# A sum moved behind a step's value products, and the outputs' halves and turn moved behind the probabilities' own

## The chip, the cores and the metric

The kernel runs on one core of a Trainium2 chip. The metric is the device time of one execution in microseconds, and a kernel's time is the median of several runs. The core has a matrix engine (TensorE, PE in the rows), a vector engine (DVE), an activation engine (ACT), a general engine (POOL), and SyncE (SP), which here does nothing but issue transfers. Each engine takes its instructions in the order in which the program gives them.

## The reference

Two stages follow each other. The first is block-sparse attention over 4 batches, 8 heads, 768 positions and a head width of 64, in blocks of 32. A block of queries sees its neighbours, the first and last block, and three sampled blocks; the first and the last block of queries see all. The second is a feed-forward stage over the 3072 x 512 result:

```python
scores = np.where(mask, scale * q @ k.T, -1e9)
attn = softmax(scores)
x = (attn @ v) as 3072 x 512
h = x @ w_in                              # 512 x 2048
g = h * erf(softplus(h))
out = g @ w_out                           # 2048 x 512
```

## The kernel before

The feed-forward products and those with the values work on halves: a float32 matrix is held as a 16-bit high half and a 16-bit low half (what the high half leaves out), and a product is made of three products of halves. Before the values of a batch can be split, they are scaled by a power of two that follows from their sum of squares.

The main loop (line 1022) has a pass for each of 96 groups of the feed-forward stage, and two more to empty it. A group is 256 tokens by 256 of the 2048 columns. Each pass, called a step here, issues for the feed-forward stage: `ff_first` (24 products, `h<-xT,wi`), `ff_logs` (five activations on ACT), `ff_gate` of the group before (DVE, makes `g`), `ff_second` of the group two before (`o<-wo,g`, 12 products) and, after the eighth group of a token block, `ff_store`, which empties the two output banks `o` into `wo`'s spare rows, one on ACT and one on DVE. Many steps also advance the attention stage by one unit (a set of queries of half the heads): `scores` (PE, into the single bank pair `s`), `soft_max` (DVE), `soft_exp` (ACT, `pf`), `soft_low` (DVE: a cast to the high half from the thirteenth unit on, and the subtraction that gives the low half of `p`) and `soft_turn` (a transposing transfer on SP's queue, `pT<-p`). Two units later `values` multiplies `pT` by gathered values `vb` into the bank `po_bank`, `norm` (DVE) scales it into `xf`, and, when both halves of the heads are there, `turn` takes over: ACT copies `xf` to a high half, DVE subtracts for the low half (`x<-xf,x`), and SP's queue turns both (`xT<-x`). `ff_first` of a later token block reads `xT`.

A batch's values are prepared while the batch before is worked on. `behind` (line 853) puts parts into a list, and the next step runs them as `ready`: a first part (`high`) early in the step and a second (`low`) late. `scale_v` (line 239) is a first part: it sums the squares over the partitions with a product by ones, `whole_sum` (line 194), and turns the sum into a scale with four small DVE instructions, `m_v`, `e_v`, `s_v`, `i_v`. `high_v` is another first part: ACT multiplies by that scale. The sum is written to the last column of the bank that `values` uses:

```python
po_bank = ps_po.tile([P, 512], F32, tag="po", name="po_bank")
whole = po_bank[:, 511:]                                    # whole_sum
po = po_bank[:, : 4 * (D + 1)].rearrange(...)               # values
```

Outside the preparation ahead of the loop `scale_v` runs six times, twice for each later batch. In five of these steps there is a `values` as well. `turn` does something in every step whose `values` completes a set of heads, 24 times in all, 22 of them with a turn on SP's queue.

Nothing reorders the program: each engine's list, SP's queue of transfers included, is what the lines give in their order.

Of the kernel before, what the change touches and what calls it, by code (L numbers as in the profile page):

```python
# [43 lines left out]
def sparse_attention_moe(ctx: ExitStack, tc: tile.TileContext, qT, kT, v, sampled, w_in, w_out, out):  # L44
# [125 lines left out]
    def transpose(out, x):  # L170

        if not on_pe[0]:
            sp.dma_start_transpose(out=out, in_=x)
            return
        for k in range(0, x.shape[1] // P, 8):
            t = ps_o.tile([P, 512], F32, tag="o", name="turned").bitcast(F16).rearrange("p (k c) -> p k c", c=P)
            for j in range(8):
                c = (k + j) * P
                pe.transpose(t[:, j], x[:, c : c + P], unity)
            act.activation(out[:, k : k + 8], t, AF.Copy)  # L180
# [73 lines left out]
    def write_values():  # L254
        for write in writes:
            sp.dma_start(*write)
        writes.clear()
# [272 lines left out]
    def work(steps):  # L530

        for step in steps.split():
            kind, key, k = step[0], step[1], step[2:]
            steps_of[kind](key, *([int(k)] if k else []))
# [42 lines left out]
    def soft_turn(unit):  # L577

        p2, _, _, n = softs.pop(unit)
        tag = "_".join(str(x) for x in unit)  # L580
        if unit[0] == "e":
            pT = at.tile([P, 8, P], F16, tag="pe", name=f"pT_{tag}", bufs=1)
        else:
            pT = at.tile([P, 16, P], F16, tag="pT", name=f"pT_{tag}", bufs=3)[:, : 2 * n // P]
        transpose(pT, p2)
        pts[unit] = pT
# [109 lines left out]
    def turn(b, t, quad):  # L696
        if quad == 1:
            xf = xfs.pop((b, t))
            x2 = at.tile([P, 2, DM], F16, tag="x2", name=f"x2_{b}_{t}", bufs=1)
            xr = xf.rearrange("p h d -> p (h d)")  # L700
            act.activation(x2[:, 0], xr, AF.Copy)
            dve.tensor_tensor(x2[:, 1], xr, x2[:, 0], ALU.subtract)
            ch, u = divmod(t, CT)
            if u == 0:
                xTs[b, ch] = mo.tile([P, 2 * NK, CT, P], F16, tag="xT", name=f"xT_{b}_{ch}", bufs=3)
            transpose(xTs[b, ch][:, :, u, :], x2.rearrange("p a s -> p (a s)"))
# [20 lines left out]
    def ff_first(b, ch, fg):  # L727
        tag = f"{b}_{ch}_{fg}"
        isg = first_scale(b)
        h = ps_h.tile([P, W], F32, tag="h", name=f"h_{tag}")  # L730
        xT = xTs[b, ch].rearrange("p n u c -> p n (u c)")
        for j in range(FG):
            f = fg * FG + j
            hj = h[:, j * CW : (j + 1) * CW]
            for kt in range(NK):
                i, c = (f // 4) * NK + kt, (f % 4) * P
                hi, lo = wi16[:, i, c : c + P], wi16[:, i, 512 + c : 512 + c + P]
                xa, xb = xT[:, kt], xT[:, NK + kt]
                pe.matmul(hj, hi, xa, start=kt == 0, stop=False)
                pe.matmul(hj, hi, xb, start=False, stop=False)  # L740
                pe.matmul(hj, lo, xa, start=False, stop=kt == NK - 1)
        ffs[b, ch, fg] = (h, isg)
# [3 lines left out]
    def ff_logs(b, ch, fg):  # L746

        h, isg = ffs[b, ch, fg]
        tag = f"{b}_{ch}_{fg}"
        x = mo.tile([P, W], F32, tag="x", name=f"x_{tag}")  # L750
        act.activation(x, h, AF.Relu, bias=H_CAP, scale=isg)
        act.activation(x, x, AF.Exp, bias=H_CAP, scale=-1.0)
        act.activation(x, x, AF.Ln, bias=1.0, scale=C0)
        q = mo.tile([P, W], F32, tag="s", name=f"q_{tag}", bufs=2)
        act.activation(q, x, AF.Square, bias=C2)
        act.activation(x, x, AF.Ln, bias=1.0, scale=C4)
        ffs[b, ch, fg] = (h, x, q)

    def ff_power(b, ch, fg):
        h, x, q = ffs[b, ch, fg]  # L760
        dve.scalar_tensor_tensor(q, x, C3 / C1, q, ALU.mult, ALU.add)
# [5 lines left out]
    def ff_gate(b, ch, fg):  # L767
        h, _, hs = ffs.pop((b, ch, fg))
        scale = 2.0**-H_SHIFT
        dve.scalar_tensor_tensor(hs, hs, -1.0, h, ALU.add, ALU.mult)  # L770
        g = mo.tile([P, 2, W], F16, tag="g", name=f"g_{b}_{ch}_{fg}", bufs=FF_LAG + 1)
        dve.tensor_scalar(g[:, 0], hs, scale, None, ALU.mult)
        dve.scalar_tensor_tensor(g[:, 1], hs, scale, g[:, 0], ALU.mult, ALU.subtract)
        gs[b, ch, fg] = g
# [34 lines left out]
    def write_results():  # L809
        for result in results:  # L810
            sp.dma_start(*result)
        results.clear()
# [14 lines left out]
    def gathers(m):  # L827

        nonlocal kfree, vfree
        if kjobs and kfree >= 4 and kjobs[0][0] in have_k:  # L830
            kfree -= 4
            gather(*kjobs.pop(0))
        room = 4 if begun > 0 else VGS
        while vjobs and vjobs[0][0] in have_v:
            b, i = vjobs[0]
            n = 2 if i > 0 else 1
            fresh = b > 0 and 0 < i < VGS
            if vfree < n or room < n * (1 + fresh):
                break
            vfree -= n  # L840
            room -= n * (1 + fresh)
            vjobs.pop(0)
            gather_v(b, i) if i > 0 else whole_v(b, -1 - i)

    def next_queries(m):

        b, n = divmod(m, per)
        if n < 9 and n % 2 == 1:
            load_q(b, n // 2 + 2)
        if n == per - 1 and b + 1 < B:  # L850
            load_q(b + 1, 1)
# [38 lines left out]
    def seen(unit):  # L890

        if unit[0] == "m":
            return unit[1:]
        if unit[0] == "f" and unit[2] % 2 == 1:
            return unit[1], MT, unit[2] // 2
        return None

    def used_keys(unit):
        nonlocal kfree
        if unit[0] == "m" and unit[3] == 1:  # L900
            kfree += 4
        elif unit[0] == "e" and unit[2] == 1:
            kfree += 4
# [6 lines left out]
    def unit_of(n):  # L910
        return units[n] if 0 <= n < len(units) else None

    def values_of(place):
        nonlocal vfree
        values(*place)
        if place[2] == 1:
            vfree += 4 if place[1] < MT else 5
# [104 lines left out]
    for m in range(len(groups) + FF_LAG):  # L1022
        ch, i = divmod(m, NGR)
        steps = 0
        if ch < len(until):
            first = until[ch - 1] if ch else FIRST
            steps = first + -(-(until[ch] - first) * (i + 1) // NGR) - begun
        elif begun < len(units) + PV_LAG:
            steps = 1
        assert steps in (0, 1)  # L1030
        group = groups[m] if m < len(groups) else None
        last = groups[m - 1] if 0 < m <= len(groups) else None
        unit = unit_of(begun) if steps else None
        old = unit_of(begun - PV_LAG) if steps else None
        place = seen(old) if old and begun - PV_LAG >= FIRST else None
        begun += steps
        write_values()
        write_results()
        if group:
            ff_first(*group)  # L1040
            ff_logs(*group)
        ready, prepared[:] = prepared[:], []
        for high, _ in ready:
            if high:
                high()
        if place:
            values_of(place)
        if steps:
            gathers(begun)
        if unit:  # L1050
            scores(unit)
            used_keys(unit)
        if last:
            ff_gate(*last)
        if place:
            norm(*place)
        if m < len(EARLY):
            work(EARLY[m])
        if m >= FF_LAG:
            for u in range(CT):  # L1060
                ff_second(*groups[m - FF_LAG], u)
        if unit:
            soft_max(unit)
            next_queries(begun - 1)
        if group:
            ff_power(*group)
        for _, low in ready:
            if low:
                low()
        if unit:  # L1070
            soft_exp(unit)
        if group:
            ff_exp(*group)
        if m < len(AMID):
            work(AMID[m])
        if m >= FF_LAG:
            for u in range(CT):
                ff_store(*groups[m - FF_LAG], u)
        if place:
            turn(*place)  # L1080
        if unit:
            soft_low(unit)
            soft_turn(unit)
        if m < len(LATE):
            work(LATE[m])
        if unit:
            behind(begun - 1)
# [37 lines left out]
```

## Time and profile before

| | us |
|---|---|
| median of 3 runs | 824.81 |
| lowest and highest | 823.09, 825.76 |
| the profiled execution | 830.67 |
| its span, first to last instruction | 828.9 |
| mean granted clock of TensorE | 0.932 |

The profiled execution is one run, taken with the profiler on; its own time stands 0.7% above the median. Rows of the trace are times within its span.

### The profile page before, as it was taken

What the parts mean: (1) busy time and instruction counts of PE and PEld (TensorE: products, weight loads), DVE (VectorE), ACT (ScalarE), POOL (GpSimd) and SP (SyncE); (2) the same over time, 40 slices, a digit from 0 to 9 for tenths busy, and PEclk for the clock granted to TensorE, in tenths of its full rate; (3) what the DMA queues carried; (4) which work ended last, traced back from release to release, by engine and by line L of the source; (5) the groups of instructions that cost most, each with busy time, mean ns of one, the idle gap of its engine ahead of it and who ended that gap; (6) DMA issues with size and microseconds to landing.
All of it is one profiled execution on the core that took longest, in us unless ns stands there. A gap on an engine that the chain in (4) does not pass through costs nothing. (4 is left out here: it accounts for less than half of the span.)

```text
span 828.9 us, 26604 instructions
## 1 busy us (share of the span) xinstructions
PE 698.3 (84%) x10852; PEld 463.3 (56%) x10852; DVE 576.0 (69%) x1019; ACT 552.9 (67%) x943; POOL 126.0 (15%) x343
## 2 busy tenths in 40 slices
PE   1353645889986979899999897999999999999997
PEld 1133423555654656566666665666676665666664
DVE  3993696988755866775677876776677767754454
ACT  4553567997555757676678767667677676676774
POOL 4621030202211221010011121100111110000000
PEclk9975766999998999899999999999999999999999
DMA  8999971797598889782478899762687968220000
GB/s 306 290 278 273 252 176 32 162 213 167 143 173 191 207 194 211 146 184 63 111 181 195 176 193 231 155 123 43 163 188 168 181 115 187 41 52 20 1 26 26
DMA packets 199498, 129.24 MB, mean 156 GB/s; under 512 B 143952, under 2 KB 167120, under 8 KB 199376
## 3 DMA queue, kind: packets, MB, share of 16 engines
q1 hardware_dynamic: 195952, 115.74, 62.4%
q0 software_dynamic: 3424, 11.80, 4.5%
q8 instruction: 85, 1.39, 0.7%
q14 instruction: 37, 0.30, 0.1%
HBM read 81.52 MB, written 12.95 MB: 114 GB/s over the span
## 5 line engine op out<-in xcount | busy, mean ns | idle before, releaser
L60 PE MATMUL h<-xT,wi 128*128 128x256 f16 x2304 | 274.7, 276 | 12.0 <-ACT wi L60 5.3
L60 PE MATMUL o<-wo,g 128*128 128x512 f16 x1152 | 271.5, 386 | 7.4 <-ACT wo L60 4.0
L60 PEld LDWEIGHTS <-wi 128*128 128x128 f16 x2304 | 227.6, 99 | 64.0 <-ACT wi L60 6.5
L60 PEld LDWEIGHTS <-g 128*128 128x128 f16 x1152 | 109.3, 99 | 148.5 <-issue 33.9
L60 ACT ACTIVATE x<-x 128x512 f32<-128x512 f32 x288 | 181.5, 630 | 9.1
L60 POOL COPY keys<-keys 128x128 f32 x264 | 90.0, 391 | 287.7 <-PE s_m L60 246.8
L60 ACT ACTIVATE x<-h,isg 128x512 f32<-128x512 f32 x96 | 65.9, 686 | 95.5 <-PE h L60 95.4
L60 DVE SCALAR_TENSOR_TENSOR q<-x,q 128x512 f32<-128x512 f32 x96 | 68.0, 708 | 66.5 <-ACT x L60 66.3
L60 ACT ACTIVATE pf_m<-s_m,nb_m 128x256 f32<-128x256 f32 x160 | 62.7, 474 | 57.0 <-DVE nb_m L60 54.1
L60 PE MATMUL po_bank<-vb,pT_m 128*32 128x65 f16 (+1 forms) x3840 | 46.4, 205 | 40.7 <-DMA vb<-vtab 16.2
L60 DVE SCALAR_TENSOR_TENSOR q<-q,h 128x512 f32<-128x512 f32 x96 | 65.5, 682 | 20.2 <-ACT q L60 20.2
L60 ACT ACTIVATE q<-q 128x512 f32<-128x512 f32 x96 | 60.6, 632 | 25.6 <-DVE q L60 25.5
L60 PE MATMUL s_m<-keys,qt 64*32 64x192 f32 (+1 forms) x1600 | 70.7, 359 | 6.9 <-ACT pf_m L60 4.1
L60 DVE SCALAR_TENSOR_TENSOR g<-q,g 128x512 f16<-128x512 f32 x96 | 66.5, 692 | 3.3
L60 PEld LDWEIGHTS <-pT_m 128*32 128x32 f16 x3840 | 40.1, 101 | 50.8 <-issue 19.5
L60 DVE TENSOR_REDUCE mx_m<-s_m 128x4 f32<-128x1024 f32 x40 | 48.8, 1220 | 20.4 <-PE s_m L60 19.9
L60 ACT ACTIVATE q<-x 128x512 f32<-128x512 f32 x96 | 60.5, 630 | 3.0
L60 PEld LDWEIGHTS s_m<-keys,qt 64*32 64x32 f32 (+1 forms) x1600 | 45.8, 135 | 18.1 <-ACT pf_m L60 5.0
L60 DVE TENSOR_TENSOR p_m<-pf_m,p_m 128x1024 f16<-128x1024 f32 x40 | 49.0, 1226 | 3.2 <-ACT p_m L60 2.1
L60 DVE TENSOR_SCALAR g<-q 128x512 f16<-128x512 f32 x96 | 41.1, 428 | 3.3
L60 POOL COPY keys<-wi 128x768 f32<-128x768 f32 (+1 forms) x24 | 17.0, 737 | 167.7 <-DMA wi<-in_kT_dram 167.7
L60 DVE TENSOR_TENSOR x<-xf,x 128x512 f16<-128x512 f32 x24 | 16.8, 700 | 33.6 <-ACT x L60 33.6
(113 smaller groups left out, 533.7 us busy)
## 6 DMA issues: line engine op xcount, KB each, us to landing
vb<-vtab SPq DMA_DIRECT2D x280, 65.0 KB, 3.0
vb<-vtab SPq DMA_DIRECT2D x32, 390.0 KB, 4.4
vtab<-vn SPq DMA_DIRECT2D x16, 390.0 KB, 6.8
vb<-vtab SPq DMA_DIRECT2D x12, 520.0 KB, 5.5
vraw<-in_v_dram SPq DMA_DIRECT2D x7, 768.0 KB, 6.0
qt<-in_qT_dram SPq DMA_DIRECT2D x20, 256.0 KB, 4.3
out_dram<-wo SPq DMA_DIRECT2D x20, 256.0 KB, 4.3
vb<-vtab SPq DMA_DIRECT2D x36, 130.0 KB, 3.1
```

What stands on the lines that cost most here:

```text
L60: done = call(*args, **kwargs)
```

## The change

Two calls are moved. `values_of(place)` goes ahead of the loop over the first parts, so that on TensorE the sum for the values' scale comes behind the step's value products (DVE's and ACT's own order stays the same by this). `turn(*place)` goes behind `soft_low(unit)` and `soft_turn(unit)`: on DVE the subtraction for the outputs comes behind the cast and subtraction for the probabilities, and on SP's queue `xT<-x` behind `pT<-p`. ACT has nothing in `soft_low` and `soft_turn`, so its order stays. No instruction is added or left out.

```diff
         ready, prepared[:] = prepared[:], []
+        if place:
+            values_of(place)
         for high, _ in ready:
             if high:
                 high()
-        if place:
-            values_of(place)
         if steps:
             gathers(begun)
...
-        if place:
-            turn(*place)
         if unit:
             soft_low(unit)
             soft_turn(unit)
+        if place:
+            turn(*place)
         if m < len(LATE):
             work(LATE[m])
```

## Rows read from the trace of the kernel before

**Rows 1.** The page's first part: busy time, share, instructions.

```profile
PE 698.3 (84%) x10852; PEld 463.3 (56%) x10852; DVE 576.0 (69%) x1019; ACT 552.9 (67%) x943; POOL 126.0 (15%) x343
```

**Rows 2.** Waits: who waited for whom; total us, times, longest us.

```profile
DVE x L60 <- ACT x L60: 33.6, 24, 2.1
...
PE po_bank L60 <- DMA vb<-vtab: 16.2, 7, 8.1
...
PE po_bank L60 <- DVE m_v L60: 11.2, 6, 4.5
PE po_bank L60 <- DMA pT_m<-p_m: 10.5, 6, 3.4
```

**Rows 3.** Windows: length, busy us by engine, granted clock, DMA share, GB/s.

```profile
680.20:687.90 7.70, 7.69 (x141) 4.85 (x140) 5.65 (x10) 5.06 (x10) 0.00 (x0) 1.00 0.66 195
331.80:345.70 13.90, 10.11 (x143) 6.04 (x142) 10.11 (x23) 8.60 (x16) 0.46 (x1) 0.75 0.87 188
508.00:522.90 14.90, 10.45 (x144) 6.10 (x143) 11.08 (x23) 9.16 (x17) 1.32 (x3) 0.77 0.84 180
470.00:482.10 12.10, 9.20 (x173) 5.93 (x172) 7.61 (x14) 7.52 (x16) 3.46 (x10) 0.86 1.24 225
160.00:180.00 20.00, 17.88 (x398) 11.21 (x399) 18.45 (x29) 18.35 (x28) 1.71 (x7) 0.91 0.91 191
```

**Rows 4.** Timeline around the step at 331.8: start, length, instruction, idle before.

```profile
333.19 1.57 ACT L60 ACTIVATE pf_m<-s_m,nb_m 128x256 f32<-128x256 f32 x4 [0.93 <-DVE nb_m L60]
...
334.43 0.28 PE L60 MATMUL po_bank<-one,top_v 128*128 128x1 f32 x2
...
335.83 0.69 DVE L60 TENSOR_TENSOR x<-xf,x 128x512 f16<-128x512 f32 x1 [2.14 <-ACT x L60]
...
337.16 1.23 DVE L60 TENSOR_TENSOR p_m<-pf_m,p_m 128x1024 f16<-128x1024 f32 x1
...
338.30 0.15 DVE L60 TENSOR_SCALAR m_v<-po_bank 128x1 f32<-128x1 f32 x1
...
338.51 1.50 PE L60 MATMUL po_bank<-vb,pT_m 128*32 128x65 f16 x96 [3.79 <-DVE m_v L60]
...
342.81 0.96 DVE L60 TENSOR_REDUCE mx_f<-s_f 128x1 f32<-128x768 f32 x1 [1.34 <-PE s_f L60]
...
345.96 0.75 DVE L60 TENSOR_SCALAR wo<-o,iso 128x512 f32<-128x512 f32 x1
```

**Rows 5.** Timeline of DVE in the step at 508.0.

```profile
523.38 0.75 DVE L60 TENSOR_SCALAR wo<-o,iso 128x512 f32<-128x512 f32 x1
```

**Rows 6.** Timeline at waits for turned probabilities: SP's queue and PE.

```profile
292.90 1.24 SPq L60 DMA_TRANSPOSE xT<-x  x1
294.22 2.29 SPq L60 DMA_TRANSPOSE pT_m<-p_m  x1
...
298.80 1.22 PE L60 MATMUL po_bank<-vb,pT_m 128*32 128x65 f16 x96 [3.36 <-DMA pT_m<-p_m]
...
649.71 0.96 PE L60 MATMUL po_bank<-vb,pT_m 128*32 128x65 f16 x96 [1.22 <-DVE g L60]
...
692.48 1.09 PE L60 MATMUL po_bank<-vb,pT_m 128*32 128x65 f16 x96 [1.74 <-DMA pT_m<-p_m]
693.50 0.83 PE L60 MATMUL s_e<-keys,qt 64*64 64x64 f32 x24
```

**Rows 7.** Timeline of SP's queue and PE ahead of the second token block.

```profile
173.31 4.09 SPq L60 DMA_TRANSPOSE pT_m<-p_m  x1
...
183.57 0.71 PE L60 MATMUL h<-xT,wi 128*128 128x256 f16 x5
```

**Rows 8.** Time from issue to landing: all pT, one xT, one pT.

```profile
DMA to landing us min/median/max: 4.3/5.2/10.1
...
xT<-x SPq DMA_TRANSPOSE x1, 5.5
...
pT_m<-p_m SPq DMA_TRANSPOSE x1, 5.6
```

## The prediction

> **What bounds the kernel now.** I read the page first: TensorE (PE) is busy for 84% of the span, more than any other engine [rows 1]. A mean hides the stages, so next come the waits of each engine, then windows of one step each. A step is one pass of the main loop; it begins with its 24 products `h<-xT,wi`, and I name it by the time at which these begin. The quiet step at 680.2 (24 `h`, 96 products of `values`, 8 of a full row's scores, 12 `o`) takes 7.7 us with PE busy for 7.69 of them at full clock [rows 3]: PE sets the pace, and a step gets shorter only where PE stands still or runs slowly.
>
> PE's waits inside the loop nearly all stand before `po_bank`, that is, before the first product of `values`. They have three causes: DVE's `m_v` (11.2 us in 6 waits), the turned probabilities `pT` (10.5 us) and the gathered values `vb` (16.2 us) [rows 2]. The change touches the first two. The waits' own length is not all they cost. The step at 331.8 takes 13.9 us and that at 508.0 takes 14.9, with mean granted clocks of 0.75 and 0.77, between the two levels of 1.2 and 2.4 GHz [rows 3]: PE stands for 3.79 us [rows 4] and 4.5 us, the longest of the six [rows 2], and what follows runs slowly: the 96 products take 1.50 us [rows 4].
>
> **Part one: the sum behind `values`.** Now the order on PE is `h`, `whole_sum` (two passes, 0.28 us), `values`. The sum's column is in `po_bank`, the tile that `values` writes, so `values` waits until DVE's `m_v` has read the sum. At 338.51 the first product starts 0.06 us after `m_v` ends [rows 4]. `m_v` is late because DVE does it in order, behind the previous step's tail: it waits 2.14 us for ACT's copy of the outputs, then does x's low half (0.69) and, until 337.16 + 1.23 = 338.39, the cast and the subtraction of `p_m`, 2.56 us in all, 1.9 of them for `p_m` [rows 4].
>
> With the sum behind `values`, PE has no reader to wait for: `values` can run at 334.4, the sum at 335.4, the scores at 335.8. The scores need the exponentials that began at 333.19 to be done, four in 1.57 us, so by 334.8 [rows 4]. The step costs the quiet 7.7 plus 0.3 for the sum, 8.0. That gives 13.9 - 8.0 = 5.9 us here and 14.9 - 8.0 = 6.9 us at 508.0, which has the same form [rows 3]. Together 12.8 us, clock included.
>
> What is late next: the following step's first `o` needs the output banks, emptied by the two `wo<-o` of this step. DVE's ends at 345.96 + 0.75 = 346.7, and at 524.1 in the other step [rows 4, 5]. In the new order DVE's tail is 0.9 us shorter (part two) and the 1.34 us that DVE's `mx_f` waited for PE's scores are gone [rows 4], so these end near 344.5 and 521.9. PE gets there at 331.8 + 8.0 and 4.4 more, 344.2: 2.6 for the 24 `h` (331.8 to 334.43), 0.96 for `values` and 0.83 for an edge row's scores [rows 4, 6]. In the other step it is 520.4. New waits of 0.3 and 1.5 us: 12.8 - 1.8 = 11.0 us.
>
> The other three steps of this kind in the loop have `m_v` waits under a microsecond (the 11.2 us less 3.79 and 4.5 leave 2.9 for four, one of them ahead of the loop, where the order stays). I count nothing for them: two lie just ahead of the `pT` waits at 298.8 and 475.7, which would take back what they give, and in the third DVE is short of time. Bounds: 0 and 1.6 us. The cost of this part lies on DVE: `m_v`, and behind it the gate, `norm`, the maximum and the scale for ACT's halves, wait for `values` to end, about 1 us later where DVE was early. The gate's product is read by PE a step later, so this is hidden in a quiet step; where it is not, it costs up to 1 us, once.
>
> **Part two: `turn` behind `soft_low` and `soft_turn`.** Nothing is added or removed. On DVE the low half of `p` no longer waits behind x's: the exponentials are done at 334.8, the cast and the subtraction (1.9) end at 336.7, x's low half follows at 336.7 to 337.4, and `m_v` comes at 337.4 instead of 338.30. DVE's waits before `x` (33.6 us in 24 [rows 2]) are filled with that work. ACT's order stays the same. On SP's queue the turn of `p` is issued ahead of the turn of x.
>
> At four places PE waits for a `pT` whose issue stood right behind an `xT`: 3.36, 1.22 (put down to DVE's g there, but `pT`, issued at 644.1, lands 5.6 us later [rows 8], at that moment) and 1.74 us [rows 6], and the 2.9 us that PE is not busy in the step at 470.0 [rows 3]. The `xT` ahead holds the queue for 294.22 - 292.90 = 1.32 us [rows 6]; at the other three the same two rows are 1.32, 2.72 and 1.68 us apart. Earlier by that much, and no more than the wait itself: 1.32 + 1.32 + 1.22 + 1.68 = 5.5 us. The rest of the 10.5 us lies mostly before 180, but there DVE is busy for 18.45 of 20 us [rows 3] and gives back only its own wait before x; with the later `m_v` against it I count 1.0 us, bounds 0 and 2.2.
>
> The clock may add to this. The step at 470.0 keeps PE busy for 9.20 us where a quiet one needs 7.69 [rows 3], so slow clock costs 1.5 us after a 2.9 us stall, while after 1.22 us the products run at full speed (0.96 us for 96 [rows 6]). For the stalls of 1.6 and 2.0 us that would be left no row tells; bounds 0 and 3.0 us for both, and I take 0, since the stalls are cut and not gone. On this the Trainium skill, "TensorE: Matmul & The Clock Gate", section "What's actually happening", says that the monitor's window runs freely, not from the start of the kernel, so that equal stalls need not cost the same: by it the sum could be 1.5 or 3.0 us better.
>
> What it costs: x's turn lands later, by the turn of `p` ahead of it. The feed-forward first reads it two or more steps later nearly everywhere. The tightest is the step at 183.57: there `pT` takes the queue for 4.09 us from 173.31 [rows 7], right behind x's turn, which is issued at 172.0 and lands 5.5 us later [rows 8]; later by 4.1 it lands at 181.6, still 2 us ahead. That margin covers the early gain, not more.
>
> **Sum.** 11.0 + 5.5 + 1.0 = 17.5 us. From this I take 1.0 for the `pT` of the steps after 331.8 and 508.0: PE now comes there 5.9 us sooner, `pT` only 1.5 us. Issued near 336.8, it lands at the median of 5.2 us [rows 8] at 342.0, when PE wants it at 342.4, and the other step is alike; by the extremes (4.3 and 10.1 us) each step loses 0 or up to 5. Net 16.5 us. The profiled execution took 830.67 us (span 828.9, 1.8 around it) and would take 814.2; the median of the runs is 0.7% below it, and 824.81 - 16.5 = 808.3. I forecast 808.
>
> **The rivals.** (a) `pT` takes the place of `m_v`: in the two steps after the long stalls it lands as late as the slow ones, and each gives back about 3 us: 808 + 6 = 814. For it: the spread of the landings [rows 8]; against: 0.4 us of room at the median. Chance 0.13.
> (b) The order of issue doesn't reach the landing, since both turns run at once: the four gains of 5.5 fall away, and (a) loses its 1.5 us of help: about 815. The Trainium skill, "DMA: Bandwidth & Descriptors", section "Two DMAs through the same engine are not ordered", says that nothing orders transfers across the 16 engines; by that rule this is the case to expect. Against it, the queue's own rows: a turn's issue takes 1.24 to 4.09 us and the next begins only behind it [rows 6, 7]. Chance 0.12.
> (c) Slower: `m_v` is now behind everything that `values` waits for. Where gathers are late in such a step, the stall holds DVE's whole queue and ACT's scale too. Five steps carry a sum and `values`; above 3.3 us in each the 16.5 us are gone. The `vb` waits have a mean of 2.3 us and reach 8.1 [rows 2]; at 5.2, between the two, the kernel takes 808 + 26 = 834. For it: gathers wait on the same queue; against: in none of the five steps is a gather the last wait now. Chance 0.06.
> (d) No change: PE's place is taken by another equal wait (the output banks or the scores' bank), 824.8. The scores' bank is free in time by the rows, the output banks are in the sum. Chance 0.07.
>
> **How the numbers follow.** The forecast has 0.62. Runs of this kernel differ by 0.3%, so 0.3% is what can be told: faster means under 822.3. Forecast, (a) and (b) are faster, 0.87; (d) same, 0.07; (c) slower, 0.06. The low end adds the clock's 3.0, the small steps' 1.6, the early 1.2 and the 1.0 taken off: 801. The high end takes (a) and (b) with 5 us more for both together: 820. Cases (c) and (d) stay outside.
>
> **What the new profile would show.** Right: `DVE m_v` gone from PE's waits in the loop; the steps that held 13.9 and 14.9 us at 8 to 9.5 with the clock at 1.00; DVE's waits before `x` under 10 us; `pT` waits smaller by half. Wrong: an equal wait for `pT` or `vb` before `po_bank`, PE waiting for `wo` before `o` by more than 2 us, or PE waiting for `xT` before `h`.

## The result and the profile after

The changed kernel takes 815.0 us (median of 6 runs, 810.17 to 818.35), the kernel before 825.2 beside it (6 runs). The ratio is 0.9861 with an interval of 0.9829 to 0.9892: 11.5 us less, between 8.9 and 14.1 (differences in time are here and below the ratio's share of the median of before; the two medians differ by 10.2). The forecast was 808 in a range of 801 to 820, from a gain of 16.5 us. The side and the range were right, the gain was put too high.

The profiled execution took 814.35 us, its span is 812.6 us with a mean granted clock of 0.954 (before: 828.9 and 0.932). First the page's line of busy time, then the waits of both engines (total us, times, longest us).

```profile
PE 689.7 (85%) x10852; PEld 458.3 (56%) x10852; DVE 575.1 (71%) x1019; ACT 551.1 (68%) x943; POOL 126.5 (16%) x343
```

```profile
PE po_bank L60 <- DMA vb<-vtab: 15.5, 8, 6.6
...
PE po_bank L60 <- DMA pT_m<-p_m: 3.6, 4, 2.3
...
DVE x L60 <- ACT x L60: 3.1, 4, 1.2
...
PE s_f L60 <- ACT pf_m L60: 2.6, 2, 1.5
...
PE po_bank L60 <- DVE m_v L60: 1.3, 1, 1.3
```

Against [rows 2]: DVE's waits before `x` fell from 33.6 to 3.1 us, those of PE for `m_v` from 11.2 in 6 to one of 1.3 ahead of the loop, those for `pT` from 10.5 to 3.6. The gathers kept theirs (16.2, 15.5). One line is new: PE waits, in two steps, before a full row's scores `s_f` until ACT has done the exponentials `pf_m`. PE's busy time fell by 8.6 us [rows 1] with the same 10,852 instructions, so part of the gain is clock.

The timeline of the step that began at 331.8 before (start, length, instruction, idle before) and windows of it, of the one at 508.0 and of the one at 470.0, whose beginnings are now 326.4, 495.4 and 461.6:

```profile
317.84 1.01 SPq L60 DMA_DIRECT2D vraw<-in_v_dram  x1
...
323.32 0.84 ACT L60 ACTIVATE vj<-vraw 128x768 bf16<-128x768 f32 x1 [3.59 <-DMA vraw<-in_v_dram]
...
325.25 0.15 DVE L60 TENSOR_REDUCE top_v<-vsq 128x1 f32<-128x2 f32 x1 [4.80 <-ACT vj L60]
...
328.39 1.22 DVE L60 TENSOR_REDUCE mx_m<-s_m 128x4 f32<-128x1024 f32 x1
...
329.10 0.96 PE L60 MATMUL po_bank<-vb,pT_m 128*32 128x65 f16 x96
...
329.90 1.57 ACT L60 ACTIVATE pf_m<-s_m,nb_m 128x256 f32<-128x256 f32 x4 [0.94 <-DVE nb_m L60]
...
329.99 0.38 PE L60 MATMUL po_bank<-one,top_v 128*128 128x1 f32 x2
...
331.52 1.51 PE L60 MATMUL s_f<-keys,qt 64*64 64x512 f32 x8 [1.15 <-ACT pf_m L60]
...
332.23 1.23 DVE L60 TENSOR_TENSOR p_m<-pf_m,p_m 128x1024 f16<-128x1024 f32 x1
...
333.48 3.56 SPq L60 DMA_TRANSPOSE pT_m<-p_m  x1
...
333.97 0.15 DVE L60 TENSOR_SCALAR m_v<-po_bank 128x1 f32<-128x1 f32 x1
...
337.14 1.25 SPq L60 DMA_TRANSPOSE xT<-x  x1
...
338.83 0.96 PE L60 MATMUL po_bank<-vb,pT_m 128*32 128x65 f16 x96 [0.49 <-DVE q L60]
...
340.80 1.46 PE L60 MATMUL o<-wo,g 128*128 128x512 f16 x6 [0.25 <-ACT wo L60]
```

```profile
326.40:335.60 9.20, 8.05 (x144) 5.08 (x143) 7.79 (x18) 8.04 (x15) 1.89 (x5) 1.00 0.65 186
495.40:504.95 9.55, 8.06 (x143) 5.05 (x142) 8.14 (x18) 8.24 (x16) 1.81 (x5) 1.00 0.64 183
461.60:469.85 8.25, 7.69 (x174) 5.30 (x173) 6.74 (x13) 5.89 (x12) 1.87 (x5) 1.00 1.35 233
```

Both parts change the order as they say. `values` starts at 329.10 without a wait, 4.9 us ahead of `m_v` (in [rows 4] it began 0.06 us behind it), and `pT` is issued ahead of `xT`. The 13.9, 14.9 and 12.1 us of [rows 3] are 9.2, 9.55 and 8.25, at a clock of 1.00. What stands in the way now is read upward from 331.52: the scores wait for the exponentials (331.47), these for `mx_m` on DVE, and DVE had stood for 4.80 us before `top_v`, with `mx_m` queued behind it, because ACT's squares `vj` waited 3.59 us for the raw values `vraw`, issued at 317.84. The prediction did not look at these squares; in the step at 331.8 of before they come at 326.62 (ACT, timeline of before):

```profile
326.62 0.84 ACT L60 ACTIVATE vj<-vraw 128x768 bf16<-128x768 f32 x1 [1.47 <-DMA vraw<-in_v_dram]
```

### The profile page after: what moved, and what is told of

It reads as the page before. It is cut to its first block, busy times and chain, and to the rows that moved or that the text cites. A ratio compares the mean times of both kernels' runs of the same rounds, so it can differ in the third digit from the quotient of the medians.

```text
span 812.6 us, 26628 instructions
## 1 busy us (share of the span) xinstructions
PE 689.7 (85%) x10852; PEld 458.3 (56%) x10852; DVE 575.1 (71%) x1019; ACT 551.1 (68%) x943; POOL 126.5 (16%) x343
## 5 line engine op out<-in xcount | busy, mean ns | idle before, releaser
L60 PE MATMUL h<-xT,wi 128*128 128x256 f16 x2304 | 273.7, 276 | 13.9 <-ACT wi L60 7.4
L60 POOL COPY keys<-keys 128x128 f32 x264 | 92.0, 396 | 286.2 <-PE s_m L60 249.1
L60 PE MATMUL s_m<-keys,qt 64*32 64x192 f32 (+1 forms) x1600 | 67.5, 347 | 6.3 <-ACT pf_m L60 4.1
L60 PE MATMUL po_bank<-vb,pT_m 128*32 128x65 f16 (+1 forms) x3840 | 44.3, 202 | 22.1 <-DMA vb<-vtab 15.5
L60 DVE TENSOR_REDUCE mx_m<-s_m 128x4 f32<-128x1024 f32 x40 | 48.8, 1220 | 17.1 <-PE s_m L60 16.2
L60 PEld LDWEIGHTS <-pT_m 128*32 128x32 f16 x3840 | 38.0, 99 | 33.2 <-DMA vb<-vtab 13.9
L60 PEld LDWEIGHTS s_m<-keys,qt 64*32 64x32 f32 (+1 forms) x1600 | 44.4, 131 | 16.2 <-ACT pf_m L60 5.2
L60 DVE CAST p_m<-pf_m 128x1024 f16<-128x1024 f32 x30 | 20.9, 696 | 25.4 <-ACT pf_m L60 25.4
```

Source lines behind the costliest of these rows:

```text
L60: done = call(*args, **kwargs)
```

## The experiments

Ratios are to the kernel before on the same chip: its median there was 829.6 us (29 runs) for the first four and 830.28 (23 runs) for the next four. The last four are one profile each. "First" and "second long step" are those at 331.8 and 508.0 of before.

**Each part alone.** The kernel before with one of the diff's two moves:

```diff
# e1: values_of(place) ahead of the first parts, turn where it was
# e2: turn(*place) behind soft_turn(unit), values_of where it was
```

> The kernel before with the first part alone: the sum behind the values, the outputs' halves and turn where they were. By the theory that the two long steps (13.9 and 14.9 us) were made of the wait for m_v and of the slow clock behind it, this part alone takes 6 to 9 us off the median, m_v is gone from the waits of PE in the loop, and those two steps take 9 to 10.5 us; DVE's waits before x stay near 33 us. By the rival that pT takes the place of m_v, the steps right behind them show a pT wait of 2 us or more each and the gain is under 5 us.

> The kernel before with the second part alone: the outputs' halves and turn behind those of the probabilities, the sum where it was. By the theory of an earlier pT the median falls by 3 to 5 us, DVE's waits before x fall under 10 us, the pT waits of PE fall by half, and the two long steps stay at 12.5 to 14 us, since m_v comes only 0.9 us sooner. By the rival that the order of issue does not reach the landing, the change is under 1.5 us and the pT waits stay near 10 us in all.

The sum alone: 823.96 us, 0.9935 [0.9909, 0.9961], 5.4 us less and under the 6 to 9 expected. The turn alone: 826.06 us, 0.9959 [0.9935, 0.9982], 3.4 us less, as expected. Together 8.8, just under the interval of the whole (8.9 to 14.1); with their own intervals of about 2 us each the parts add up to the whole within the noise. With the sum alone `m_v` is gone inside the loop, and `pT` waits of 7.9 us remain. With the turn alone DVE's waits before `x` fall to 3.1 us as in the changed kernel, but the `pT` waits are not halved (waits of that kernel):

```profile
PE po_bank L60 <- DMA pT_m<-p_m: 8.3, 3, 3.0
...
PE po_bank L60 <- DVE m_v L60: 7.9, 5, 2.8
```

Both parts carry a gain, and part one about half of the 11.0 us that I gave it. Where part two gains when it is alone is not where I had expected it: the two long steps took 10.7 and 11.9 us in this profile (12.5 to 14 expected), while at three of the four places of the forecast `pT` was still awaited for 2.95, 2.64 and 2.70 us. At the second of them, the step at 470.0 of before, `pT` is issued ahead of `xT` and yet lands only 0.3 us sooner in the step (5.4 us behind its first `h`, 5.7 before). SP's queue and PE there, with the turn alone and then in the changed kernel:

```profile
454.12 9.97 SPq L60 DMA_DIRECT2D vb<-vtab  x14
...
464.71 2.95 SPq L60 DMA_TRANSPOSE pT_m<-p_m  x1
...
471.53 1.03 PE L60 MATMUL po_bank<-vb,pT_m 128*32 128x65 f16 x96 [2.64 <-DMA pT_m<-p_m]
```

```profile
448.36 8.95 SPq L60 DMA_DIRECT2D vb<-vtab  x14
...
457.92 2.81 SPq L60 DMA_TRANSPOSE pT_m<-p_m  x1
...
464.91 0.96 PE L60 MATMUL po_bank<-vb,pT_m 128*32 128x65 f16 x96 [0.56 <-DMA pT_m<-p_m]
```

In both, fourteen gathers hold the queue until just before the turn (464.09 and 457.31), and PE has its `pT` 7.4 and 7.6 us behind their end.

**The order on SP's queue alone.** The kernel before, with x's turn issued behind p's, but x's halves left ahead on DVE:

```diff
-            transpose(xTs[b, ch][:, :, u, :], x2.rearrange("p a s -> p (a s)"))
+            turns.append((xTs[b, ch][:, :, u, :], x2.rearrange("p a s -> p (a s)")))
...
             soft_turn(unit)
+        issue_turns()
```

> The kernel before with only the order on SP's queue changed: the turn of x is issued behind the turn of p, while ACT and DVE make the halves of the outputs where they did. It splits the second part in two. If the gain of the second part lies on the queue, this takes off as much as the second part alone (3 to 5 us) with DVE's waits before x still near 33 us; if it lies in DVE's order, this gives under 1.5 us.

It came out slower, and not only without a gain: 832.83 us, 1.0048 [1.002, 1.0077]. Its waits, and ACT and PE in the first long step, which begins at 329.1:

```profile
PE po_bank L60 <- DVE m_v L60: 14.7, 6, 6.3
...
PE po_bank L60 <- DMA pT_m<-p_m: 6.1, 4, 2.5
```

```profile
325.50 0.84 ACT L60 ACTIVATE vj<-vraw 128x768 bf16<-128x768 f32 x1 [3.02 <-DMA vraw<-in_v_dram]
...
337.38 1.50 PE L60 MATMUL po_bank<-vb,pT_m 128*32 128x65 f16 x96 [5.34 <-DVE m_v L60]
```

The `pT` waits shrink by 4.4 us, and those for `m_v` grow by 3.5 (to more than the 8.3 to 12.8 us of all four profiles of before): PE is at the first long step at 329.1, 2.7 us sooner than in [rows 3], and the raw values are used only 1.1 us sooner. What the queue gives, `m_v` takes back while the sum stands ahead of `values`. That the kernel is 4 us slower, and not only equal, this doesn't explain; its profiled execution was the second fastest of its twelve, with a span (826.2 us) no longer than those of before, so the rest stays open.

**Taking the new wait away.** Two kernels made from the changed one: in e4 the squares and all that follows for the second group of raw values come one unit later, in e8 the raw values are loaded ahead of the exponentials.

```diff
# e4
+                s = quad
-                if k == 1:
+                if k == 1 + s:
                     prepare(square_v, bound_v, place[:2])
-                if k == 2:
+                if k == 2 + s:
...
# e8
         if unit:
+            raw_values(begun - 1)
             soft_exp(unit)
```

> The changed kernel, with the squares, the sum and the halves of a batch's second four heads one unit later, so that the load of their raw values has a step more to land. In the changed kernel the scores of the two steps at 326.4 and 495.4 wait 1.15 and 1.49 us for the exponentials of the step before. By the theory that these are late because ACT's squares wait for the raw values (3.6 and 3.8 us) and hold the gate and the maximum on DVE, both waits go and the median falls by 2 to 4 us under the changed kernel. By the rival that DVE's own length makes them late, the waits move to the step with the sum and the median stays within 1.5 us.

> The changed kernel with the load of a batch's raw values issued earlier in its step, ahead of the exponentials and so ahead of both turns on SP's queue. By the theory that the scores of the two long steps wait because ACT's squares wait for this load (3.6 and 3.8 us) and hold DVE's gate and maximum, the squares' wait falls under 1 us, the waits of 1.15 and 1.49 us go, and the median falls by 2 to 4 us under the changed kernel. By the rival that DVE's own work is as late without it, those waits stay above 0.7 us and the median is within 1.5 us.

The scores' waits are gone in both, so late raw values were their cause. But nothing is won, where 2 to 4 us were expected: 818.68 us, 0.9866 [0.9826, 0.9907], and 821.58 us, 0.99 [0.985, 0.9949]. The rows of SP's queue, DVE and PE tell why, first in e4 behind the second long step, then in e8 behind the first:

```profile
500.09 8.28 SPq L60 DMA_DIRECT2D vb<-vtab  x11
...
502.14 1.23 DVE L60 TENSOR_TENSOR p_m<-pf_m,p_m 128x1024 f16<-128x1024 f32 x1
...
508.46 4.61 SPq L60 DMA_TRANSPOSE pT_m<-p_m  x1
...
515.14 1.50 PE L60 MATMUL po_bank<-vb,pT_m 128*32 128x65 f16 x96 [3.57 <-DMA pT_m<-p_m]
```

```profile
326.31 8.50 SPq L60 DMA_DIRECT2D vb<-vtab  x11
...
330.95 1.23 DVE L60 TENSOR_TENSOR p_m<-pf_m,p_m 128x1024 f16<-128x1024 f32 x1
...
334.90 4.56 SPq L60 DMA_TRANSPOSE pT_m<-p_m  x1
...
342.19 0.96 PE L60 MATMUL po_bank<-vb,pT_m 128*32 128x65 f16 x96 [2.86 <-DVE g L60]
```

`p_m` is ready at 503.4 and 332.2, but eleven gathers hold the queue until 508.4 and 334.8, so `pT` is issued 5.1 and 2.7 us late, and PE waits 3.57 and 2.86 us a step later (the second wait is put down to `g`, but it ends 7.3 us behind the issue of `pT`). This is rival (a), and it appears in these two kernels, where the new wait is removed. Neither beat the changed kernel.

**The change, and the kernel before, once more; and the queue's order put back.** e5 is the changed kernel, e6 the kernel before. e7 is the changed kernel with `turn` between the two:

```diff
             soft_low(unit)
-            soft_turn(unit)
         if place:
             turn(*place)
+        if unit:
+            soft_turn(unit)
```

> The changed kernel once more, beside the kernel before on this chip, for a second profile of it. The time is that of before less 9 to 13 us. The two steps that hold the sum and a full row's scores stay at 9 to 10 us; if their waits of 1.15 and 1.49 us for the exponentials are a property of the program and not of one execution, they are there again within 0.5 us. By the rival that most of the 16.3 us between the first two profiles is the scatter of the transfers, the span is within 5 us of 812.6 and the waits for pT and vb differ from the first profile by several us in single steps.

> The kernel before once more, for a second profile and for the scatter of a comparison with itself. Ratio 1.000 within 0.003. The two long steps are there again with m_v waits of 3 to 6 us each; the waits for pT at four places move by up to 2 us each. By the theory that the first profile was a slow execution of this kernel, its span here is 4 to 6 us under 828.9 on a chip of the same speed.

> The changed kernel with the old order on SP's queue: the halves of the outputs are made behind the low half of p, but the turn of x is issued ahead of the turn of p. Undoes the queue's part of the second move and keeps DVE's. By the theory that the gain lies in DVE's order, it is within 2 us of the changed kernel; by the theory that pT ahead of xT is worth 1.3 to 2.7 us at each of four places, it is 4 to 7 us slower than the changed kernel, with pT waits of 8 us or more in all.

The change again: 817.28 us, 0.9875 [0.9825, 0.9924], 10.4 us less. The scores' wait is there again in the second long step (1.73 us, the step took 12.06) and not in the first, which took 7.95 us: it belongs to the execution as much as to the program. The kernel before against itself: 1.0008 [0.9979, 1.0038]. With the queue's order back: 826.56 us, 0.9957 [0.9927, 0.9987], so that 6.8 of the 10.4 us (some 2 to 12 by the two intervals) go with two calls in another order. Its waits for `pT`, and SP and PE behind the first long step:

```profile
PE po_bank L60 <- DMA pT_m<-p_m: 14.7, 9, 3.9
```

```profile
336.56 1.26 SPq L60 DMA_TRANSPOSE xT<-x  x1
...
337.87 4.50 SPq L60 DMA_TRANSPOSE pT_m<-p_m  x1
...
344.51 0.96 PE L60 MATMUL po_bank<-vb,pT_m 128*32 128x65 f16 x96 [1.22 <-DMA pT_m<-p_m]
```

14.7 us in 9 waits where the changed kernel has 0.9 (e5) to 3.6: the order of issue does reach the landing, and rival (b) doesn't hold as it was put. How far the order reaches is taken up below.

The second profile of before has a span of 822.6 us, 6.3 less than the first, `m_v` waits of 2.20 and 3.32 us in the long steps where 3 to 6 were expected, and its two long steps with their followers (two steps each) take 36.5 us instead of 42.9. Four more profiles follow.

**How long are the long steps?** Both kernels unchanged and the sum alone, one profile each:

> The kernel before once more, for the length of its two long steps with their followers (24 h to 24 h, two steps each). Theory one (part one's 11.0 us was read from an execution whose two long steps were unusually long): the pairs at about 326 to 333 and 500 to 508 take 16 to 20 us each, 34 to 39 us in sum as in the second profile (36.5), with the m_v waits there at 2 to 3.5 us. Theory two (the first profile was the usual case, the second the odd one): the sum comes out at 41 to 44 us (first profile: 42.9), with m_v waits of 3.5 us or more.

> As the run ahead of this one, a further execution of the kernel before. Theory one: 34 to 39 us for the two pairs of steps; theory two: 41 to 44 us. If the two executions fall on either side, the length of these steps varies from execution to execution and one profile can't size the term.

> Part one alone (the sum behind the values), a second profile. Theory one: the two pairs stay near the 35.9 us of its first profile, 34 to 37, so that part one gives 1 to 4 us there and not 11. Theory two: 31 to 34 us, 8 to 11 less than the 42 of the kernel before.

> The whole change, a third profile. Theory one: the two pairs at 33 to 36 us (34.3 and 33.9 in the first two), with the wait of a full row's scores for the exponentials of 1 to 1.7 us in at least one of the two long steps; PE waits for m_v nowhere in the loop. Theory two: 30 to 33 us, at least one long step at the quiet 8.0.

Lengths in us, from the beginning of the long step's `h` to that of the step after its follower:

| kernel, profiles | first | second | both |
|---|---|---|---|
| before (first, e6, e9, e10) | 21.0, 17.1, 18.4, 23.0 | 21.9, 19.3, 21.9, 22.4 | 42.9, 36.5, 40.3, 45.4 |
| sum alone (e1, e11) | 16.4, 16.5 | 19.5, 19.9 | 35.9, 36.4 |
| changed (first, e5, e12) | 17.0, 14.9, 16.0 | 17.3, 19.0, 17.7 | 34.3, 33.9, 33.7 |

For the two kernels with the sum behind `values` theory one came true; for the kernel before neither did (e9 falls between what the two expected, e10 above both). Its sums scatter over 9 us, theirs by about half a microsecond. So narrow a scatter of two and three sums is partly chance, since the single lengths differ by up to 2.1 us. What scatters in the kernel before is the raw values. ACT, DVE and PE in the first long step, in e6 (it begins at 332.5) and in e10 (332.6):

```profile
325.76 0.83 ACT L60 ACTIVATE vj<-vraw 128x768 bf16<-128x768 f32 x1
...
337.43 0.15 DVE L60 TENSOR_SCALAR m_v<-po_bank 128x1 f32<-128x1 f32 x1
...
337.63 0.95 PE L60 MATMUL po_bank<-vb,pT_m 128*32 128x65 f16 x96 [2.20 <-DVE m_v L60]
```

```profile
329.08 0.84 ACT L60 ACTIVATE vj<-vraw 128x768 bf16<-128x768 f32 x1 [3.15 <-DMA vraw<-in_v_dram]
...
340.91 0.15 DVE L60 TENSOR_SCALAR m_v<-po_bank 128x1 f32<-128x1 f32 x1
...
341.11 1.50 PE L60 MATMUL po_bank<-vb,pT_m 128*32 128x65 f16 x96 [5.62 <-DVE m_v L60]
```

The squares start 3.3 us later, `m_v` 3.5 and `values` 3.5. In all ten long steps of the order before (four profiles and e3) `m_v` ends 11.8 to 12.0 us behind the start of the first `vj`; with the turn alone it is 10.8, twice, which is the 1.0 us that the second move gives there. The stall for `m_v` has two parts, then: in the ten steps it is 2.0 to 2.5 us longer than ACT's own wait for the raw values, which runs from 0 to 4.0 us, and the first part is there even when the raw values are in time (e6 above). Where the scores wait in the changed order (e1, e7, e11 and the changed kernel, eight steps), they start 8.2 to 8.3 us behind it. With the second long step of e11:

```profile
502.95 0.84 ACT L60 ACTIVATE vj<-vraw 128x768 bf16<-128x768 f32 x1 [5.51 <-DMA vraw<-in_v_dram]
...
511.14 2.83 PE L60 MATMUL s_f<-keys,qt 64*64 64x512 f32 x8 [1.74 <-ACT pf_m L60]
```

So the change doesn't take PE off the raw values: it shortens the way from them to PE by some 3.6 us, and hangs it on a product that comes 1.3 us later in the step (at 3.9 us, `values` at 2.6 to 2.7). Where the raw values are later still, `values` waits as well: in the second long step of e5 and e11, with waits of 4.85 and 5.51 us before `vj`, it waited 0.59 and 1.19 us for `xf`, which on DVE stands behind the same squares.

## Why the prediction was right, and why its size was off

**The two long steps (11.0 us forecast): right mechanism, mis-sized.** `m_v` is gone, and the first long step alone took 7.95 us in both profiles of the sum alone, as the 8.0 of the forecast say. But the sum alone gives 5.4 us in time, and 41.25 - 36.13 = 5.1 us between the means of the table's last column. Two steps of the working failed. The first is "the scores' bank is free in time by the rows": the exponentials were taken at the place they had in that step, as if they moved up with PE. They hang from the raw values, which follow PE's gain only in part: between [rows 4] and the new profile PE comes to the first long step 5.4 us sooner, its `vj` only 3.3 (326.62 by the row of before, 323.32). In the second long step the sum alone met a wait of 1.6 and 1.7 us there, and the step took 11.3 and 12.3 us instead of 8.0, at a clock of 0.85 and 0.86. The followers of the long steps gave back 2.3 us more (16.4 us for both, 14.1 before), with waits of 1.41 and 1.50 us for `pT` behind the first; the second move makes these smaller. The forecast had named the scores' bank in rival (d) and priced it at nothing. The second is the last line of the sum, "824.81 - 16.5 = 808.3". The stalls were read from an execution of 830.67 us, 5.9 above that median, and much of such an excess can sit in the very stalls that the change removes: over the four profiles of before, spans of 822.6, 828.9, 829.0 and 830.2 us go with 36.5, 42.9, 40.3 and 45.4 us in these steps. Of the 2.75 us that this term is short (below), 1.65 are the 42.9 us that I read against the mean of 41.25, and 1.1 are the changed kernel's 34.0 us against the 32.9 that I expected of it. Against its own execution the sum gave 814.2, and the profiled execution of the changed kernel took 814.35; the others took 813.79 and 817.84. That the first agrees so well is in part luck, as the single places below show.

**The output banks (1.8 us taken off):** 0.25 and 0.40 us in the new profile, at most 0.7 in one step of the others. Where the scores wait, that wait stands ahead of them and gives ACT and DVE the time. Where PE comes later against the same squares there is no wait at all: in e5 the first long step begins 3.4 us later than in the new profile, `vj` at the same 323.32, and the step and its follower take 7.95 and 6.96 us.

**`pT` ahead of `xT` (5.5 us): right in sum, not in mechanism.** The four steps whose waits began the argument took 44.45 us in the mean of the four profiles of before and 37.65 in the three of the changed kernel: 6.8 less. But it isn't the order of the two turns alone that did it, for with the turn alone they took 44.6 us (one profile). The step that failed is "Earlier by that much, and no more than the wait itself". At these places gathers end on SP's queue just ahead of the two turns. Counted from their end, `pT` landed after 6.6, 7.9, 8.2 and 8.8 us where `xT` went first, and after 5.4, 7.5, 7.8 and 7.7 us where `pT` did (means of seven profiles each; where no landing is recorded, the end of PE's wait stands for it): 1.2, 0.4, 0.4 and 1.1 us sooner, 3 us in all. The rest of an earlier issue was lost on the way to the landing. What else the changed kernel gains at 470.0 comes with the gathers: they end 4.2 to 4.3 us ahead of the step's `h`, 1.8 to 3.1 in the kernel before, 2.0 with the turn alone, 3.1 and 3.5 with the sum alone. Why it takes both moves isn't shown.

Place by place the forecast was less exact than its sum, and that the sum came out is luck: 2.0 for the step with the wait at 298.8 (1.3 forecast), 3.6 at 470.0 (1.3), nothing at 649.7 (1.2; the step scatters from 8.3 to 13.5 us before and from 8.5 to 11.7 after) and 1.2 at 692.5 (1.7). Of the surplus of 2.3 at 470.0 some 1.5 is clock, which I had put at 0 with bounds to 3.0: [rows 3] have 0.86 there, the new window 1.00, and PE is busy for 7.69 us instead of 9.20. The rest is a shorter wait. The 1.0 us for the early stretch came out at 0.8 (73.56 to 72.75 us in the mean for the steps from 138.7 to 212.3).

**x's later turn (no cost forecast).** No wait before `h` in the loop is put down to a turn of x in the three profiles of the changed kernel. One wait that no row explains, in the step at 183.57 of before, is 0.6 to 1.4 us there and was 2.1.

**The sum.** 41.25 - 34.0 = 7.25 for the long pairs (10.0 forecast, with the 1.0 for their followers taken off), 6.8 and 0.8 make 14.9 us where I had 16.5. The spans of these profiles differ by 827.7 - 813.6 = 14.1. The timed medians say 10.4 to 11.5 with intervals up to 14.5, so a few executions with a profile are still a coarse sample.

**The rivals.** The 815 looks like (a), 814, but its mechanism is not what the time lost: in the new profile PE waited only 0.49 and 0.34 us before `values` behind the long steps. (b) doesn't hold as it was put, since e7 is slower, but the order reached the landing by 3 us and not by 5.5. (c) did not come: no step with a sum waits for a gather, and `m_v` began 4.9 us behind the start of `values` without PE waiting for it. (d) came in small: a wait on the scores' bank, but of 1.7 us at most and not of 3.8 and 4.5.

## What to carry to other kernels

A wait that is removed uncovers the next reader of the same late source: follow the chain up to the transfer that starts it, and price the new order by the fixed distance from there (here 8.2 instead of 11.8 us behind the first square), not by the place in the step. A step that is long because of a late transfer varies from execution to execution; a gain read from one profile is set against that execution's own time, not taken off a faster median. Two issues on one queue are worth ordering by who is needed first, but together with the work that feeds them: the queue's order alone cost 0.5% here, and was worth 0.8% with the rest. Read the gain at the landing and not at the issue: of the 5.5 us that I counted from the issue, 3 reached the landing.

## What the runs showed of the hardware

Equal stalls cost unequal time. In the first long step PE stood for 2.20 us in e6 and 2.18 in e9, and in both the clock had been at the upper level since 306. Windows of these steps, in this order, and of the 3.2 us behind the stall in e9 (the third figure from the end is the granted clock):

```profile
332.50:342.60 10.10, 7.90 (x143) 5.23 (x142) 7.68 (x18) 7.50 (x15) 0.00 (x0) 1.00 0.96 195
```

```profile
331.40:342.85 11.45, 9.27 (x144) 5.87 (x143) 8.12 (x19) 7.83 (x15) 0.00 (x0) 0.85 0.92 188
336.40:339.60 3.20, 3.17 (x100) 1.86 (x101) 2.82 (x9) 2.08 (x4) 0.00 (x0) 0.50 0.99 304
```

After the same stall the clock stayed at the upper level once. The other time it stood at the lower one (0.50, 1.2 GHz) right behind the stall, its mean over the step fell to 0.85, and the same products took 1.37 us more of PE's time (9.27 against 7.90). The scores' wait in the second long step does likewise between two kernels: 1.61 us in e1 with a mean clock of 0.85, 1.74 us in e12 with 1.00. What a stall of 2 us costs can't be read from one execution, then. That agrees with the Trainium skill, "TensorE: Matmul & The Clock Gate", section "What's actually happening", by which the monitor's window runs freely and is not reset when a kernel starts.
